# Sliding-window attention and a four-expert mixture: twenty units of the first layer, in place of nine, computed with tokens on partitions

## The chip, the cores and the metric

The kernel runs on one core of a Trainium2 chip. The metric is the device time of one execution in microseconds (us). Three executions of the kernel before took 355.09, 355.31 and 355.94 us; their median is 355.31 us.

## The reference, cut to what matters

```python
B, H, S, D = 4, 8, 768, 64                        # batches, heads, tokens, head width
scores = q @ k.transpose(0, 1, 3, 2) / sqrt(D)
keep   = (pos_k < 4) | ((pos_q - pos_k >= 0) & (pos_q - pos_k < 128))   # 4 sinks, a window of 128
a      = softmax(where(keep, scores, -1e9))
x      = (a @ v).transpose(0, 2, 1, 3).reshape(3072, 512)
p      = domain_probs / (domain_probs.sum(-1) + 1e-9)                   # 3072 x 4
for e in range(4):                                # every token goes through every expert
    out += p[:, e] * (relu(x @ w1[e]) @ w2[e])    # w1: 512 x 1024, w2: 1024 x 512
```

Everything arrives in fp32; the kernel computes its products in bf16 and adds them up in fp32.

## The kernel before, in words

The 3072 tokens are cut into twelve pairs (b, g): batch b (0 to 3), and g (0 to 2) for 256 tokens of it. For each pair there is attention for four pairs of heads, and then the mixture for four experts. A pair and one expert make a unit (b, g, e), 48 of them.

**The first layer.** x @ w1 of a unit is 512 inputs, 1024 outputs and 256 tokens. Most units ("fast" ones, from a start per expert in `START`, all of batches 1 to 3) do it with seven block products in place of eight (a Strassen-Winograd scheme): the operands are cut in halves both ways, and P1, P5, P6, P2, P7, P3 and P4 (the order in which they are issued, `UNITS`) are products of 256 inputs, 512 outputs and 128 tokens. The sums of weight blocks stand in `vf` (`weight_form1`), those of token blocks in `T` (`tokens`); partial sums go through three PSUM banks X, Y and V, with copies on ScalarE (ACT: `seed`, `keep`) and additions on VectorE (DVE).

There are two forms of such a product. In `emit_fast` the weight block is stationary and 128 tokens stream: eight matmuls of 128 columns. The result has hidden units on partitions, and the gate (ReLU times the expert's share of each token) is one DVE instruction with a row of gates that was broadcast to all partitions by a DMA (`gates`, 128 KB, `load_gate`). In `emit_turning` the token block is stationary and 512 weight columns stream: two matmuls of 512 columns, with tokens on partitions. The gate is then one number for each partition (`own_gates`), taken by one DVE instruction, or by two on ACT (ReLU, then a scaling). The result has to be turned before the second layer: when both parts of a half are gated, SyncE (SP) issues a DMA transpose of 128 x 1024 bf16 from a resting tile into H; a unit has two halves, so two transposes. In the kernel before, nine units of the last batch take this form: `TURNED_UNITS = (2, 1)` leaves out the first two and the last one of that batch's twelve. Their resting tiles are taken over from buffers of attention once attention is done (`widened`).

**The second layer** (`emit_product`, line 1463) uses a seven-product scheme as well: for each pair, P1, P2, P6, P5, P7, P3 and P4 over the four experts, four matmuls of 256 columns each; two PSUM banks, emptied by ACT and DVE, stored by SP. P1 and P2 read H itself, P6, P5, P7, P3 and P4 partly sums of its quarters, formed on DVE (`chore`). Units ahead of their expert's start compute the first layer by plain products (line 1092), and pairs (0, 0) and (0, 1) the second layer (line 1549).

**The order of the work.** A planner in the kernel writes out one order for every engine while the program is built. It keeps a clock for each engine (`t`), advances it by modelled durations (`pe`, `act`, `dve`, `sp`), and at each step takes, among the steps that are ready, that with the lowest priority number: an attention step, a product of the first layer, one of the second. Constants such as `SHARE_OF`, `LEAD`, `LOW_PRODUCT` and `FORM` weigh them. Each engine runs its instructions strictly in that order and waits for semaphores where data are missing. Attention of batch b+1 runs among the mixture of batch b. POOL issues the loads of q, k, v and the weights, SP the gates, the transposes and the stores.

Other places that the change touches: `load_v` at the start of the program (line 310; four blocks of the values, issued on POOL ahead of w1 of expert 0, which comes in four quarters, line 323); the division of attention's output by its row sums (lines 790 to 802: four ACT instructions of 64 columns for two heads, or one DVE instruction, line 793, for batch 0); `load_gate` (line 468).

Of the kernel before, what the change touches and what calls it, by code (L numbers as in the profile page):

```python
# [9 lines left out]
ALU = mybir.AluOpType  # L10
AX = mybir.AxisListType
FP32 = mybir.dt.float32
BF16 = mybir.dt.bfloat16
# [3 lines left out]
def kernel(  # L17
# [12 lines left out]
    nc = tc.nc  # L30
# [27 lines left out]
    ]  # L58

    NGATE = 4  # L60
    TURN_ABOUT = 0
# [12 lines left out]
    MASK = 5000  # L74
    GATE = 800
    GATE0 = 300
    FORM = 8000
    TOKEN = 3000
    MARGIN = 0
    HOLD = 0  # L80
    FULL = 7
    STEP0 = 0.01
    READY = 40
    REST = 1500
    LANDS = 0
    WIDE = 2
    OPEN = 2.5
    SOON = 28000
    NEARLY = 2
    ROWED = 24000  # L90
    GATED = 38000
# [306 lines left out]
    def form1_due(e):  # L398
        n = formed1.get(e, 0)
        if e == E - 2 and not (loaded and out_sb):  # L400
            return False
        return landed.get(("w1", e), 1e12) + 3000 < t["pe"] and (n < 3 or n == 3 and not left1[e])

    def form_due(e):
        n = formed.get(e, 0)
        if e == E - 1 and spared_at.get("w2", 1e12) > t["pe"]:
            return False
        return landed.get(("w2", e), 1e12) + 14000 < t["pe"] and (n < 3 or n == 3 and e in used)

    forming = []  # L410

# [38 lines left out]
        dve(2800, 0.0)  # L450

    gate_sb = {}

    def load_gates():

# [284 lines left out]
    def values(b, hp, g):  # L740
# [47 lines left out]
        def run(engine):  # L788
            R = sb.tile([P, 2, 2, 1], FP32, name="R", tag="R", bufs=6)
            nc.vector.reciprocal(out=R, in_=od[:, :, :, D:DX])  # L790
            at = dve(4, fixed=171)
            if b < ONACT:
                nc.vector.tensor_mul(  # L793
                    o[:, :, hp].rearrange("p q (h d) -> p q h d", h=2), od[:, :, :, 0:D], R.to_broadcast([P, 2, 2, D]),
                )
                scaled(dve(2 * P))
                return

            def multiply(engine):
                for qi in range(2):  # L800
                    for ph in range(2):
                        nc.scalar.mul(o[:, qi, hp, ph * D:(ph + 1) * D], od[:, qi, ph, 0:D], R[:, qi, ph])  # L802
# [140 lines left out]
    class Mixture:  # L943


        def __init__(self):
# [34 lines left out]
        def room(self):  # L981
            if self.units and self.units[0] in self.turning and self.halves() < 2:
                return False
            return self.spare or self.live < NH

        def halves(self):
            return sum(x[0] <= t["pe"] + REST for x in self.resting)

# [3 lines left out]
        def widened(self):  # L992

            x = sb.tile([P, 2, NHP, S], BF16, name="qkT", tag="qkT", bufs=1)
            x = x.rearrange("p i h n -> p (i h n)")
            n = 2 * QF * 2 * P
            self.spare = [x[:, i * n:(i + 1) * n].rearrange("p (k f t n) -> p k f t n", k=2, f=QF, t=2) for i in range(3)]
            for tag, bufs, n in (("qkn", NQB, 3), ("onat", 2, 2), ("aT", 4, 1)):
                self.resting += [(t["pe"], sb.tile([P, QF, 2, P], BF16, name="rest", tag=tag, bufs=bufs)) for _ in range(n)]

        def opened(self, b, g, e):

# [10 lines left out]
            def complete(at):  # L1013
                self.H_at[b, g, e] = at
                self.finished.add((b, g, e))
                if (b, g) >= PAIRS[0]:
                    self.waiting.append((b, g, e))
                    load_gates()

            self.H_part[b, g, e] = join(4, complete)  # L1020
            return {"unit": (b, g, e), "fast": fast, "left": list(UNITS) if fast else list(range(QF)), "at": {}}
# [237 lines left out]
        def emit_turning(self, u, m, ready):  # L1259
# [45 lines left out]
            c5 = X[1].rearrange("p f t n -> p (f t n)").bitcast(FP32).rearrange("p (f n) -> p f n", f=QF)  # L1305

            def gated(k, s, src, ready, slack, slot=None, then=None):
                gate = own_gates[:, 2 * g + s, e:e + 1]

                def run(engine):  # L1310
                    if engine == "act":
                        nc.scalar.activation(out=src, in_=src, func=AF.Relu)
                        act(n)
                        nc.scalar.mul(X[k][:, :, s], src, gate)
                        at = act(n)
                    else:
                        nc.vector.tensor_scalar(out=X[k][:, :, s], in0=src, scalar1=0.0, scalar2=gate, op0=ALU.max, op1=ALU.mult)
# [259 lines left out]

    own_gates = consts.tile([P, 2 * NG, E], FP32, name="own_gates")  # L1580
    own_sum = consts.tile([P, 2 * NG], FP32, name="own_sum")

    own_steps = []

    def own_load():
        nc.sync.dma_start(out=own_gates, in_=moe_domain_probs[(B - 1) * S:].rearrange("(t p) e -> p t e", p=P))
        sp()

    def own_made():
# [4 lines left out]
            lambda: nc.vector.tensor_mul(own_gates, own_gates, own_sum[:, :, None].to_broadcast([P, 2 * NG, E])),  # L1594
        ]

        def run(engine):
            steps.pop(0)()
            dve(2 * NG * E)
            own_steps.append(1)  # L1600
            if steps:
                later("dve", t["dve"], 5000, run)
# [30 lines left out]
    while mix.more() or att.more():  # L1633
# [31 lines left out]
        if turns and (ahead < 2 or not mix.second) and landed.get(("qk", *turns[0]), 1e12) < now and (turns[0][0] <= ahead or turns[0][0] == ahead + 1 and not att.todo):  # L1665
# [14 lines left out]
            next_form()  # L1680
        if ahead + 1 < B and not att.more() and (ahead == 0 or (ahead + 1, 0) in turned_at) and (ahead == 0 or mix.done >= sum(work[:ahead]) * LEAD[ahead - 1]):
            ahead += 1
            if ahead == B - 2:
                own_load()
            elif ahead == B - 1:
                own_made()
            att = Attention(ahead)
            upto = mix.done
# [78 lines left out]
```

## Time and profile before

| | |
|---|---|
| median of three executions | 355.31 us |
| the profiled execution: its time | 355.08 us |
| the profiled execution: span from first to last instruction | 353.1 us |
| TensorE (PE) busy | 347.8 us, 98% |
| VectorE (DVE) busy | 295.9 us, 84% |
| ScalarE (ACT) busy | 185.9 us, 53% |
| GpSimd (POOL) busy | 73.7 us, 21% |
| granted TensorE clock | 1.00 throughout |

A row of the groups view has the line, the engine, the operation, its tiles and shapes and its count; then the busy time in us and the mean of one in ns; then the time for which the engine stood idle just before, and what ended that. A matmul's duration counts from its start to the end of its result, so that consecutive matmuls overlap; what one costs the stream is read from the chain of work, where a piece has a start, a length and a number of instructions. The windows view has, for each stretch, the busy time of each engine, the granted clock, the mean share of the DMA engines and the GB/s that they moved.

### The profile page before, as it was taken

To read this page: it belongs to the slowest core of one execution; us is meant where nothing else is said; L and a number is where in the kernel's file an instruction comes from. 1 tells how busy PE (TensorE), PEld (TensorE's weight loads), DVE (VectorE), ACT (ScalarE), POOL (GpSimd) and SP (SyncE) were. 2 spreads that over 40 slices of the span, in tenths; PEclk is the share of its full clock that TensorE was granted. 3 is DMA by queue.
4 is the path that set the end of the run, shared out by engine and by line. 5 is a ranking of instruction groups with operands and counts; after the bars stand their busy time and mean duration, and the time that the engine had idled before them with its cause. 6 is when DMAs were issued, how large, how long until landed. Compare 5 with 4: busy or idle time off the path is not lost.

```text
span 353.1 us, 10221 instructions
## 1 busy us (share of the span) xinstructions
PE 347.8 (98%) x4184; PEld 286.2 (81%) x4184; DVE 295.9 (84%) x690; ACT 185.9 (53%) x459; POOL 73.7 (21%) x91
## 2 busy tenths in 40 slices
PE   8999999999999999999999999999999999999996
PEld 3685769756799998998999898998899675677886
DVE  6787999968999999799899899899789788567640
ACT  5773723438784453647453345555445768826111
POOL 8966114330446206000152000000000000000000
PEclk9999999999999999999999999999999999999999
DMA  9999999999999999810999910131210474736211
GB/s 172 174 190 193 221 217 183 174 159 179 155 142 166 117 197 107 110 63 8 121 158 172 130 53 11 51 88 32 51 59 23 52 121 106 164 89 107 45 62 59
DMA packets 138619, 41.32 MB, mean 117 GB/s; under 512 B 120916, under 2 KB 134580, under 8 KB 138572
## 3 DMA queue, kind: packets, MB, share of 16 engines
q0 software_dynamic: 79104, 17.31, 56.5%
q1 hardware_dynamic: 58412, 22.84, 35.6%
q8 instruction: 32, 0.52, 0.6%
q10 hardware_dynamic: 1056, 0.52, 0.6%
q14 instruction: 15, 0.12, 0.1%
HBM read 39.82 MB, written 6.34 MB: 131 GB/s over the span
## 4 chain that ended last, share of the span: by engine, by line
PE 94%; DVE 2%; DMA 2%; ACT 1%; issue 0%; ACTq 0%; DVEq 0%
PE acc L1463 35%; PE cps L1182 28%; PE acc L1549 8%; PE cps L1294 8%; PE hps L1092 7%; PE sps L697 3%; PE od L763 3%; DMA kraw<-in_k_dram 2%; PE od L756 1%; DVE aT L731 1%; DVE onat L793 1%; PE tx L821 1%; PE tr L594 0%; DVE T L1148 0%; PE sinks L658 0%; ACT aT L722 0%
## 5 line engine op out<-in xcount | busy, mean ns | idle before, releaser
L1463 PEld LDWEIGHTS <-H 128*128 128x128 bf16 x708 | 65.4, 98 | 9.2 <-issue 1.6
L1182 PEld LDWEIGHTS <-w 128*128 128x128 bf16 x992 | 61.5, 98 | 2.3
L722 ACT ACTIVATE aT<-sps 128x512 bf16<-128x512 f32 (+1 forms) x96 | 47.0, 574 | 22.6 <-PE sps L697 22.4
L1463 PE MATMUL acc<-w,H 128*128 128x256 bf16 x420 | 54.9, 273 | 0.0
L1215 DVE SCALAR_TENSOR_TENSOR H<-cps,gates 128x512 bf16<-128x512 f32 x81 | 54.3, 679 | 0.2
L1182 PEld LDWEIGHTS <-vf 128*128 128x128 bf16 x744 | 45.4, 98 | 1.9 <-issue 0.8
L802 ACT ACTIVATE onat<-od,R 128x64 bf16<-128x64 f32 x144 | 33.4, 325 | 17.9 <-DVE R L790 17.6
L1182 PE MATMUL cps<-T,w 128*128 128x128 bf16 x496 | 37.6, 219 | 0.0
L1182 PE MATMUL cps<-xT,w 128*128 128x128 bf16 x496 | 37.3, 219 | 0.0
L1182 PE MATMUL cps<-T,vf 128*128 128x128 bf16 x496 | 36.2, 219 | 0.0
L1463 PEld LDWEIGHTS <-S 128*128 128x128 bf16 x320 | 30.4, 98 | 4.7 <-issue 0.3
L1092 PE MATMUL hps<-xT,w 128*128 128x256 bf16 x256 | 31.8, 273 | 0.1
L1524 ACT COPY osb<-acc 128x256 f32<-128x256 f32 x35 | 13.1, 376 | 35.3 <-PE acc L1463 35.2
L310 POOL DMA_DIRECT2D vx<-in_v_dram x24 | 21.4, 897 | 45.2 <-PE od L763 34.4
L1549 PE MATMUL acc<-w,H 128*128 128x512 bf16 x128 | 29.9, 379 | 0.0
L1228 ACT COPY cps<-cps 128x512 f32<-128x512 f32 x31 | 18.3, 589 | 21.8 <-PE cps L1182 8.4
L1463 PE MATMUL acc<-wf,H 128*128 128x256 bf16 (+1 forms) x216 | 29.0, 271 | 0.0
L1092 PEld LDWEIGHTS <-w 128*128 128x128 bf16 x256 | 24.1, 98 | 4.6 <-issue 0.9
L1235 DVE TENSOR_TENSOR cps<-H,cps 128x512 f32<-128x512 f32 x29 | 20.0, 688 | 7.6 <-PE cps L1182 7.5
L245 POOL DMA_DIRECT2D qkn<-in_q_dram x22 | 19.6, 892 | 22.0 <-DMA qkT<-qkn 13.8
L716 DVE TENSOR_TENSOR aT<-aT,mask 128x1024 bf16<-128x1024 bf16 (+1 forms) x36 | 22.7, 636 | 1.4 <-ACT aT L722 1.3
L1549 PEld LDWEIGHTS <-H 128*128 128x128 bf16 x128 | 12.3, 98 | 12.2 <-issue 0.2
(143 smaller groups left out, 607.1 us busy)
## 6 DMA issues: line engine op xcount, KB each, us to landing
w<-in_moe_w_dram POOLq DMA_DIRECT2D x6, 1024.0 KB, 18.5
out_dram<-osb SPq DMA_DIRECT2D x17, 256.0 KB
gates<-gate_rows SPq DMA_DIRECT2D x31, 128.0 KB
vx<-in_v_dram POOLq DMA_DIRECT2D x24, 128.0 KB, 7.1
qkn<-in_q_dram POOLq DMA_DIRECT2D x22, 128.0 KB, 7.7
qkn<-in_k_dram POOLq DMA_DIRECT2D x22, 128.0 KB, 8.1
w<-in_moe_w_dram POOLq DMA_DIRECT2D x4, 256.0 KB, 7.6
w<-in_moe_w_dram POOLq DMA_DIRECT2D x2, 512.0 KB, 10.9
```

The lines of the kernel that those rows point to most:

```text
L245: nc.gpsimd.dma_start(out=both[:, i], in_=src[b, :, tb * P:(tb + 1) * P, :].rearrange("h p d -> p h d"),)
L310: nc.gpsimd.dma_start(out=vx[tb][:, :, 0:D], in_=v[b, :, tb * P:(tb + 1) * P, :].rearrange("h p d -> p h d"),)
L716: nc.vector.tensor_mul(a, a, m[:, None, :].to_broadcast([P, 2, w]))
L722: nc.scalar.activation(out=a[:, ph], in_=sps[ph][:, 0:w], func=AF.Exp, scale=scale)
L802: nc.scalar.mul(o[:, qi, hp, ph * D:(ph + 1) * D], od[:, qi, ph, 0:D], R[:, qi, ph])
L1092: nc.tensor.matmul(h[:, i].rearrange("p (q n) -> p q n", q=2), lhsT=w1_sb[e][:, db, fb * P:(fb + 1) * P], rhs=xT[b, g][:, :, db], start=(i ...
L1182: nc.tensor.matmul(y[:, f], lhsT=A[:, d, f * P:(f + 1) * P], rhs=T[:, d], start=(m in ("P1", "P5") and f == 0 and d == 0), stop=(d == 1), ...
L1215: nc.vector.scalar_tensor_tensor(out=dst, in0=src, scalar=0.0, in1=gate, op0=ALU.max, op1=ALU.mult)
L1235: nc.vector.tensor_add(tiles["V"], c5, tiles["X"])
L1294: nc.tensor.matmul(y.rearrange("p f n -> p (f n)"), lhsT=T[:, d], rhs=A[:, d], start=(m in ("P1", "P5") and d == 0), stop=(d == 1), skip_g ...
L1463: nc.tensor.matmul(y, lhsT=self.operand(b, g, e, m)[:, f], rhs=forms[e][m][:, f, cs], start=(k == 0 and f == 0 and m in (("P1", "P5", "P2" ...
L1549: nc.tensor.matmul(op, lhsT=H[:, fb // QF, fb % QF, s], rhs=w2_sb[e][:, fb, :], start=(fb == 0), stop=(fb == NFB - 1),)
```

## The change

Twenty units take the tokens-on-partitions form instead of nine: of the 24 units of batches 2 and 3 all but the first four, that is, all of pairs (2, 1) to (3, 2). `own_gates` covers two batches. The gate tiles become two fixed tiles, which serve as resting tiles after the last unit that needs broadcast gates, (2, 0, 3); three more resting tiles come from the q and k buffers as soon as the last batch's q and k are transposed, which is now before attention is over. On ACT the ReLU and the scaling of a gate become two entries of the planner. The division in attention may go to DVE for batches 2 and 3. At the start, the first quarter of w1 is issued between the third and the fourth block of the values. The order of experts changes for five pairs, and some twenty of the planner's constants get other values.

```diff
-    TURNED_UNITS = (2, 1)
-    EXPERTS = {(2, 2): (2, 0, 3, 1)}
+    TURN_ABOUT = 1
+    OWN = 2
+    TURNED_UNITS = (4, 0)
+    EXPERTS = {(1, 0): (0, 2, 1, 3), (1, 1): (3, 2, 1, 0), (1, 2): (3, 2, 1, 0), (2, 2): (2, 0, 3, 1), (3, 1): (3, 2, 1, 0)}
...
-    SHARE_OF = (0.96, 0.92, 0.94)
-    LEAD = (1.01, 1.0)
+    SHARE_OF = (1.01, 0.92, 0.96)
+    LEAD = (1.01, 0.99)
...
-    LOW_PRODUCT = 2.7
+    LOW_PRODUCT = 2.9
...
-    FORM = 8000
+    FORM = 6000
...
-    REST = 1500
+    REST = 3000
...
-    ALONE = 1.3
+    ALONE = 2.0
-    CHORES = 4
+    CHORES = 3
...
+    gate_tiles = [consts.tile([P, 2, 2, P], FP32, name=f"gates{i}") for i in range(NGATE // 2)]
...
-        x = mo.tile([P, 2, P], FP32, name="gates", tag="gates", bufs=NGATE)
+        i = len(gate_sb) % NGATE
+        x = gate_tiles[i // 2][:, i % 2]
...
-    load_v(0, (2, 3))
+    load_v(0, (2,))
     load_w1(0, 4, [0])
+    load_v(0, (3,))
     load_w1(0, 4, [1])
...
             def multiply(engine):
+                if engine == "dve":
+                    nc.vector.tensor_mul(
+                        o[:, :, hp].rearrange("p q (h d) -> p q h d", h=2), od[:, :, :, 0:D], R.to_broadcast([P, 2, 2, D]),
+                    )
+                    scaled(dve(2 * P))
+                    return
...
-            later("act", at, 600, multiply)
+            later("any" if b >= SHARED else "act", at, 600, multiply)
...
-            mine = [u for u in self.order if u[0] == B - 1]
+            mine = [u for u in self.order if u[0] >= OWN]
             self.turning = set(mine[TURNED_UNITS[0]:len(mine) - TURNED_UNITS[1]])
...
+        def rest_gates(self):
+            for x in gate_tiles:
+                self.resting.append((t["pe"], x.rearrange("p i t n -> p (i t n)").bitcast(BF16).rearrange("p (f t n) -> p f t n", f=QF, t=2)))
...
                     if engine == "act":
                         nc.scalar.activation(out=src, in_=src, func=AF.Relu)
-                        act(n)
-                        nc.scalar.mul(X[k][:, :, s], src, gate)
-                        at = act(n)
-                    else:
-                        nc.vector.tensor_scalar(out=X[k][:, :, s], in0=src, scalar1=0.0, scalar2=gate, op0=ALU.max, op1=ALU.mult)
-                        at = dve(n, fixed=152)
+
+                        def scaled(engine):
+                            nc.scalar.mul(X[k][:, :, s], src, gate)
+                            done(act(n))
+                        later("act", act(n), SCALED, scaled)
+                        return
+                    nc.vector.tensor_scalar(out=X[k][:, :, s], in0=src, scalar1=0.0, scalar2=gate, op0=ALU.max, op1=ALU.mult)
+                    done(dve(n, fixed=OWNED_READ))
...
-        nc.sync.dma_start(out=own_gates, in_=moe_domain_probs[(B - 1) * S:].rearrange("(t p) e -> p t e", p=P))
+        nc.sync.dma_start(out=own_gates, in_=moe_domain_probs[OWN * S:].rearrange("(t p) e -> p t e", p=P))
...
+            if b == B - 1 and x[1] == NQB - 1:
+                mix.rest("qkn", NQB, 3, turned_at[x])
```

More of the change, by code (lines that the diff above doesn't have):

```diff
@@ L76 @@
     GATE0 = 300
-    FORM = 8000
+    FORM = 6000
     TOKEN = 3000
-    MARGIN = 0
+    MARGIN = 500
     HOLD = 0
     FULL = 7
-    STEP0 = 0.01
+    STEP0 = 0.03
     READY = 40
-    REST = 1500
+    REST = 3000
     LANDS = 0
+    SCALED = 300
+    SHARED = 2
+    MARGIN1, MARGIN2 = 4000, 14000
+    OWNED_READ = 215
     WIDE = 2
     OPEN = 2.5
-    SOON = 28000
+    SOON = 24000
     NEARLY = 2
@@ L401, in form1_due @@
             return False
-        return landed.get(("w1", e), 1e12) + 3000 < t["pe"] and (n < 3 or n == 3 and not left1[e])
+        return landed.get(("w1", e), 1e12) + MARGIN1 < t["pe"] and (n < 3 or n == 3 and not left1[e])
     def form_due(e):
@@ L407, in form_due @@
             return False
-        return landed.get(("w2", e), 1e12) + 14000 < t["pe"] and (n < 3 or n == 3 and e in used)
+        return landed.get(("w2", e), 1e12) + MARGIN2 < t["pe"] and (n < 3 or n == 3 and e in used)
     forming = []
@@ L984, in room, with rest @@
             return self.spare or self.live < NH
+        def rest(self, tag, bufs, n, at):
+            self.resting += [(at, sb.tile([P, QF, 2, P], BF16, name="rest", tag=tag, bufs=bufs)) for _ in range(n)]
+        def rest_gates(self):
+            for x in gate_tiles:
+                self.resting.append((t["pe"], x.rearrange("p i t n -> p (i t n)").bitcast(BF16).rearrange("p (f t n) -> p f t n", f=QF, t=2)))
         def halves(self):
@@ L997, in widened @@
             self.spare = [x[:, i * n:(i + 1) * n].rearrange("p (k f t n) -> p k f t n", k=2, f=QF, t=2) for i in range(3)]
-            for tag, bufs, n in (("qkn", NQB, 3), ("onat", 2, 2), ("aT", 4, 1)):
-                self.resting += [(t["pe"], sb.tile([P, QF, 2, P], BF16, name="rest", tag=tag, bufs=bufs)) for _ in range(n)]
+            self.rest("onat", 2, 2, t["pe"])
+            self.rest("aT", 4, 1, t["pe"])
         def opened(self, b, g, e):
@@ L1018, in complete @@
                     load_gates()
+                    if not TURNED_UNITS[1] and self.gated[-1] == (b, g, e):
+                        self.rest_gates()
             self.H_part[b, g, e] = join(4, complete)
@@ L1307, in gated @@
             def gated(k, s, src, ready, slack, slot=None, then=None):
-                gate = own_gates[:, 2 * g + s, e:e + 1]
+                gate = own_gates[:, 2 * ((b - OWN) * NG + g) + s, e:e + 1]
                 def run(engine):
@@ L1576, in emit_second @@
                     used.add(e)
-    own_gates = consts.tile([P, 2 * NG, E], FP32, name="own_gates")
-    own_sum = consts.tile([P, 2 * NG], FP32, name="own_sum")
+    OWNED = 2 * NG * (B - OWN)
+    own_gates = consts.tile([P, OWNED, E], FP32, name="own_gates")
+    own_sum = consts.tile([P, OWNED], FP32, name="own_sum")
     own_steps = []
     def own_load():
-        nc.sync.dma_start(out=own_gates, in_=moe_domain_probs[(B - 1) * S:].rearrange("(t p) e -> p t e", p=P))
+        nc.sync.dma_start(out=own_gates, in_=moe_domain_probs[OWN * S:].rearrange("(t p) e -> p t e", p=P))
         sp()
@@ L1682 @@
             ahead += 1
-            if ahead == B - 2:
+            if ahead == 1:
                 own_load()
-            elif ahead == B - 1:
+            elif ahead == 2:
                 own_made()
```

6 lines of the change are left out of this document (3 added, 3 removed).

## The prediction

> **What bounds the kernel now.** I read the page first (busy times, slices, the chain that ended last), then the groups of PE alone, then the chain between two times, then the windows.
>
> ```profile
> span 353.1 us, 10221 instructions
> PE 347.8 (98%) x4184; PEld 286.2 (81%) x4184; DVE 295.9 (84%) x690; ACT 185.9 (53%) x459; POOL 73.7 (21%) x91
> PE   8999999999999999999999999999999999999996
> ...
> PE 94%; DVE 2%; DMA 2%; ACT 1%; issue 0%; ACTq 0%; DVEq 0%
> ...
> L1463 PE MATMUL acc<-w,H 128*128 128x256 bf16 x420 | 54.9, 273 | 0.0
> L1182 PE MATMUL cps<-T,w 128*128 128x128 bf16 x496 | 37.6, 219 | 0.0
> ```
>
> The matmul stream is the kernel: 94% of the chain is PE, and the last number of the group rows, idle time ahead of them, is 0.0. The windows show where PE is not full.
>
> ```profile
> core 0: us, PE busy (x) PEld busy (x) DVE busy (x) ACT busy (x) POOL busy (x), PEclk, DMA share, GB/s
> 0.00:23.00 23.00, 20.58 (x225) 13.30 (x226) 16.89 (x69) 15.84 (x35) 20.74 (x29) 1.00 1.59 180
> 93.00:165.00 72.00, 72.00 (x1031) 65.70 (x1030) 68.51 (x163) 41.01 (x116) 22.48 (x27) 1.00 1.22 121
> 203.00:235.00 32.00, 32.00 (x472) 29.43 (x470) 29.47 (x65) 16.85 (x45) 0.00 (x0) 1.00 0.15 44
> 235.00:264.00 29.00, 29.00 (x426) 26.68 (x424) 25.50 (x56) 15.31 (x42) 0.00 (x0) 1.00 0.20 56
> 264.00:290.00 26.00, 26.00 (x274) 20.25 (x272) 23.17 (x55) 16.49 (x38) 0.00 (x0) 1.00 0.43 63
> 290.00:327.00 37.00, 37.00 (x282) 25.17 (x280) 26.45 (x55) 23.90 (x45) 0.00 (x0) 1.00 0.57 116
> 327.00:353.10 26.10, 23.26 (x232) 20.84 (x229) 10.53 (x28) 3.69 (x11) 0.00 (x0) 1.00 0.18 54
> ```
>
> From 93 to 327 us PE is busy in every microsecond of the quoted stretches, at clock 1.00. Idle time is left only in the first 23 us (2.4 us) and behind the last matmul (2.8 us). So a time can get shorter only by fewer or cheaper matmuls, or at the start; and a wait that the change adds to PE lengthens it, because none is there to be replaced.
>
> **The change, part by part.**
>
> *The eleven further turned units.* The two forms of a product, from the chain (start, length, instructions):
>
> ```profile
> 55.42 8.04 PE cps L1182 x144
> ...
> 279.95 3.88 PE cps L1294 x18
> ...
> 286.00 4.37 PE acc L1463 x40
> ...
> 292.10 3.90 PE cps L1294 x18
> ```
>
> Line 1182 makes 18 products of eight matmuls in 8.04 us, 0.447 each. Line 1294 makes nine products of two matmuls in 3.88 to 3.90 us, 0.431 to 0.433 each. The difference is 0.014 to 0.016 us. Eleven units of seven products are 77 products: 616 matmuls go and 154 come, a saving of 1.05 to 1.2 us; I take 1.15. All of it lies on the path. It is small because the columns streamed are the same, 1024 for a product; only the small cost of a matmul is paid two times instead of eight. (A second-layer product is 4.37 / 10 = 0.437 us, used below.)
>
> The Trainium skill, TensorE: Matmul & The Clock Gate, section Back-to-back issue gap, gives as sustained spacing about 81 ns for 128 columns and 131 ns for 512. By that a product would fall from 0.65 to 0.26 us and the change save some 30 us (an estimate from that page). The trace disagrees, with 56 ns (8.04 / 144) and 216 ns (3.88 / 18), which is near the same section's formula for an isolated matmul.
>
> *What the other engines get.* Durations:
>
> ```profile
> L1215 DVE SCALAR_TENSOR_TENSOR H<-cps,gates 128x512 bf16<-128x512 f32 x81 | 54.3, 679 | 0.2
> L1317 DVE TENSOR_SCALAR rest<-cps,own_gates 128x512 bf16<-128x512 f32 x9 | 6.7, 747 | 1.4 <-PE cps L1294 1.1
> L1317 DVE TENSOR_SCALAR rest<-rest,own_gates 128x512 bf16<-128x512 f32 x9 | 4.3, 480 | 0.1
> L1312 ACT ACTIVATE cps<-cps 128x512 f32<-128x512 f32 x18 | 10.5, 586 | 8.4 <-PE cps L1294 8.2
> L1314 ACT ACTIVATE rest<-cps,own_gates 128x512 bf16<-128x512 f32 x18 | 12.4, 687 | 0.6
> L802 ACT ACTIVATE onat<-od,R 128x64 bf16<-128x64 f32 x144 | 33.4, 325 | 17.9 <-DVE R L790 17.6
> L793 DVE TENSOR_TENSOR onat<-od,R 128x256 bf16<-128x256 f32 x12 | 5.1, 424 | 0.4
> ```
>
> Counted in the built order of the changed kernel: 44 broadcast gates go from DVE (44 x 0.68 = 29.9 us), 5 gates from PSUM (3.7) and 11 from SBUF (5.3) come, and 9 divisions (3.8): 17 us less. ACT gets 28 ReLUs (16.4) and 28 scalings (19.2) and loses 36 divisions (11.7): 24 us more. The new units lie between about 203 and 327 us, where the windows sum to 72.6 us of ACT and 104.6 of DVE in 124. With all the shifts put there, ACT reaches about 97 (78%) and DVE 88 (71%). Neither becomes the bound, and PE gains nothing from a freer DVE, because it does not wait for it now. Priced at nothing; if ACT's queue backs up for a while, the wait comes out in the transposes below.
>
> *Transposes.* 22 more on SP (18 become 40), 11 gate loads fewer. A transpose waits on SP for its gates; behind it in the queue stand stores, which PE does not wait for, and the next transposes, which it does: a weight load of H waits for its half, and all of PE behind it. What a turned unit's way takes, from the last one of before:
>
> ```profile
> 321.90 0.59 PE L1294 MATMUL cps<-vf,xT 128*128 128x512 bf16 x2
> ...
> 323.22 0.59 PE L1294 MATMUL cps<-w,T 128*128 128x512 bf16 x2
> ...
> 323.86 3.37 SPq L1275 DMA_TRANSPOSE qkT<-rest  x2
> ...
> 327.50:328.00 0.50, 0.50 (x6) 0.44 (x5) 0.45 (x1) 0.00 (x0) 0.00 (x0) 1.00 1.10 209
> 328.00:328.50 0.50, 0.50 (x7) 0.45 (x5) 0.45 (x1) 0.00 (x0) 0.00 (x0) 1.00 1.08 198
> 328.50:329.00 0.50, 0.50 (x7) 0.44 (x6) 0.50 (x3) 0.00 (x0) 0.00 (x0) 1.00 0.07 12
> ```
>
> P3 starts at 321.90 and P4 at 323.22, so they have been streamed by 322.33 and 323.65; the second transpose has been issued by 327.23, and the DMA share falls to 0.07 at 328.5. So the later half is there about 4.9 us behind the end of P4 (to 5.4 with the window's width); the earlier half, 1.3 us of issue ahead, about 3.6 behind P4 or 4.9 behind P3.
>
> How long may it take? In the changed PE order I counted the matmuls between a unit's P4 and its first use in the second layer, and weighed them with the lengths above. For the last unit of each pair from (2, 1) to (3, 2), P1 comes 7.1, 8.2, 10.4, 10.4 and 3.9 us behind P4; before, the turned unit with the least distance, (3, 2, 2), had 14.9. P1 needs the earlier half, P2, 1.75 us later, the other. So for (3, 2, 3), 3.9 against 3.6 and 5.7 against 4.9: just enough, with 0.3 to 0.8 us to spare; the others have more. I price it at 0; the ends are 0 and 2.5 us (below).
>
> *The start.* Rows around the first read of w1:
>
> ```profile
> 7.42 1.76 POOL L310 DMA_DIRECT2D vx<-in_v_dram  x2
> 9.16 3.16 POOL L323 DMA_DIRECT2D w<-in_moe_w_dram  x4
> ...
> DMA to landing us min/median/max: 6.6/6.6/6.6
> ...
> 15.79 0.68 PE L697 MATMUL sps<-qkT 64*128 64x128 bf16 x6
> 16.40 0.39 PE L573 MATMUL acc<-lent 128*128 128x256 bf16 x2
> 16.63 1.04 PE L1092 MATMUL hps<-xT,w 128*128 128x256 bf16 x8
> ...
> 17.93 0.23 PE L756 MATMUL od<-vsd,sinkA 128*128 128x130 bf16 x1
> ...
> 17.60 2.15 ACT L722 ACTIVATE aT<-sps 128x512 bf16<-128x512 f32 x4
> ```
>
> The first quarter (issued at 9.16, landed 6.6 later, 15.8) moves ahead of one block of values, 1.76 / 2 = 0.88 us earlier: 14.9. The fourth block is issued one quarter's 0.79 us later and lands near 15.7; its first reader is behind 17.93, so that costs nothing. The changed order puts the first group of line 1092 straight behind the sinks, drops the two idle products of 16.40 (0.23 us) and joins two single score steps into a pair. But the value products wait for ACT's exponentials, which end at 19.75 either way. So the gain lies between 0 and about 0.5 us (the idle products and one more switch); I take 0.2. A quarter that lands later than 14.9, with PE now waiting for it at 15.8 and no idle product in between, could cost 0.3.
>
> *At nothing:* the planner's constants and the experts' order. The matmul counts of attention and of the second layer are unchanged, and so is the number of blocks of score matmuls (30). PE's full stretch hides changes of place; without that cover each late operand would be paid in full. Sooner resting tiles and the two fixed gate tiles wait for regions, not for a whole tile; their first uses wait for loads as before.
>
> *The sum.* Against the profiled execution (355.08, its span 353.1 and 1.98 around it): 355.08 - 1.15 - 0.2 = 353.73. The median of the runs lies 0.23 above it: 353.96, so 354.0.
>
> **The rivals.**
>
> *Slower: the turned halves come late.* Place: the weight loads of P1 and P2 of the last unit of a pair, (3, 2, 3) above all. For it speaks that both of its last gates are on ACT (1.27 us a gate in place of 0.75 on DVE), that SP is strictly in order, and that it has waited long ahead of a transpose:
>
> ```profile
> L1275 SPq EVENT_SEMAPHORE x18: 17/17/4142, 273.4 to 325.9; - x18
> ```
>
> Were 4.1 us put into the way of (3, 2, 3), 4.9 + 4.1 stands against 5.7, 3.3 us late; with 0.4 at (2, 1), where 9.0 meets 8.9, the time is 354.0 + 3.7 = 357.7, and with half of it 355.8. It decides from 2.4 us late (355.31 + 1.07 - 354.0), that is, a way of 8.1 us. Against it: no store stands between those two transposes and the unit's P4 in SP's order. Chance 0.17.
>
> The Trainium skill, Advanced Engine Details and Errata, section X-Bar Transpose (TRN2), expects 350 to 400 GB/s, by which one transpose of 256 KB moves in about 0.7 us (an estimate). The trace has 198 to 209 GB/s, so the way is not that short here.
>
> *No difference.* The start gives nothing, since ACT ends it, and small waits of 0.1 to 0.3 us at a few of the new first reads eat half of the 1.15: 355.31 - 0.6 = 354.7, with 354.3 to 355.3 around it. For it speaks how little there is to gain; against it, that PE now waits at none of the first reads of nine units, though these have 14.9 us and more. Chance 0.25.
>
> *Far faster.* What a product costs is set by its number of matmuls, each with a weight load, and not by its columns: at line 1182's 0.056 us, 462 fewer are worth 25.8 us, and the time is 329.5. The nine turned units of before speak against it: they are in the new form already, and take 0.216 us a matmul. Chance 0.01. The rule cited above from the Trainium skill's page on TensorE is of this kind and would end near 325 us.
>
> **How the numbers follow.** The forecast (353.4 to 354.2) has 0.57, and the rest is above. A change of 0.3%, 1.07 us, is about what can be told from none; the forecast, 1.3 us, is only just beyond it. Faster 0.57 + 0.01 = 0.58, same 0.25, slower 0.17. The range goes from 353.1 (both gains at their upper ends, 1.2 and 0.5, and 0.5 for smaller waits at switches) to 356.6, where the lateness is some 2.6 us; outside lie the worse half of the slow case and little below.
>
> **What would show it.** Lines move: 1182, 1294, 1463 and 1092 become 1205, 1317, 1490 and 1115. Right: 280 matmuls in line 1317, two in 0.432 us, and 1120 in line 1205; PE full in all windows up to its last products; line 1115 first near 15.8. Wrong: idle time ahead of line 1490's weight loads, released by a DMA into H or qkT, most of all near the end; or ACT above 90% of the windows from 203 on, with gates late there.

## The result, and the profile after

| | before | changed |
|---|---|---|
| median of twelve executions each, side by side | 355.14 us | 354.32 us (354.01 to 354.58) |
| the profiled execution: its time | 355.08 us | 354.29 us |
| its span | 353.1 us | 352.6 us |
| its last matmul starts at | 350.04 us | 349.18 us |

The ratio is 0.9973 with a 95% interval of 0.9964 to 0.9981: 0.82 us less, where the forecast was 354.0 and 1.3 us less. The gain is clear of the noise, but it stays just inside the 0.3% that the prediction called no change. The last matmul starts 0.86 us earlier, yet the span is only 0.5 us shorter: from that start to the last instruction it takes 3.4 us in place of 3.1, and why was not looked into. All ratios compare fast executions alone; only e5_w2at4 and e6_t2w4, below, had slow ones, two of six each, which their medians include.

From the page of the changed kernel: the span, the busy times, the shares of the chain that ended last, and three groups.

```profile
span 352.6 us, 9354 instructions
...
PE 346.6 (98%) x3720; PEld 266.8 (76%) x3720; DVE 283.0 (80%) x671; ACT 209.6 (59%) x479; POOL 74.4 (21%) x91
...
PE 75%; DMA 20%; POOL 4%; issue 0%; ACT 0%; DVE 0%; POOLq 0%; SPq 0%
...
L816 ACT ACTIVATE onat<-od,R 128x64 bf16<-128x64 f32 x108 | 24.9, 325 | 11.4 <-DVE R L798 11.1
...
L1338 ACT ACTIVATE rest<-cps,own_gates 128x512 bf16<-128x512 f32 x36 | 24.8, 692 | 0.7
...
L1317 PE MATMUL cps<-w,T 128*128 128x512 bf16 x80 | 23.8, 379 | 0.0
```

Each form sits in the program as forecast: 80 matmuls in this group of line 1317 (280 in the line), none waiting, and 36 divisions fewer on ACT. DVE lost 13 us (forecast 17) and ACT gained 24 (forecast 24). New is the chain that ended last: 20% of it is DMA, where before it was 2%. One wait of 0.25 us at 86.7 us, shown below, is enough to lead it back into the loads. The windows, with the columns of the prediction's:

```profile
93.00:165.00 72.00, 72.00 (x1026) 65.39 (x1025) 69.21 (x167) 41.06 (x116) 23.32 (x26) 1.00 1.23 118
...
203.00:235.00 32.00, 32.00 (x317) 23.27 (x315) 25.50 (x58) 20.85 (x48) 0.00 (x0) 1.00 0.32 67
235.00:264.00 29.00, 29.00 (x246) 19.26 (x244) 23.22 (x54) 21.50 (x42) 0.00 (x0) 1.00 0.52 105
264.00:290.00 26.00, 26.00 (x198) 17.41 (x197) 19.64 (x52) 21.02 (x41) 0.00 (x0) 1.00 0.76 134
290.00:327.00 37.00, 37.00 (x257) 24.89 (x255) 23.30 (x50) 27.26 (x50) 0.00 (x0) 1.00 0.55 111
```

PE is full in these windows from 93 to 327 us, as before, and ACT is at 81% in its fullest one (21.02 of 26). The only wait of PE that the waits view names between 23 us and the end is this (engine, tile and line, releaser; us in total, times, longest); the timeline shows its place:

```profile
PE sinks L666 <- DMA qkT<-qkn: 0.2, 1, 0.2
```

```profile
86.71 0.29 PE L666 MATMUL sinks<-qkT,ksd 128*32 128x256 bf16 x4 [0.25 <-DMA qkT<-qkn]
```

Three places of the kernel before:

```profile
86.66 0.29 PE L658 MATMUL sinks<-qkT,ksd 128*32 128x256 bf16 x4
...
160.91 0.62 PE L697 MATMUL sps<-qkT 64*128 64x128 bf16 x12
...
349.87 0.39 PE L1463 MATMUL rest<-qkn,qkT 128*128 128x128 bf16 x4
```

and two of the changed kernel:

```profile
161.19 0.62 PE L705 MATMUL sps<-qkT 64*128 64x128 bf16 x12
...
349.01 0.39 PE L1490 MATMUL rest<-qkn,H 128*128 128x128 bf16 x4
```

Before, the sinks of batch 1 started at 86.66, with no wait. So these two executions are level there, although that of the changed kernel had run 0.67 us ahead at its first sinks (14.76 against 15.43; over all profiles these start at 14.7 to 14.8 or at 15.2 to 15.5 us, in programs that are the same up to there, too). The score steps of the two kernels follow one another in the same order up to 161 us. Between 86.7 and 161.2 us the changed kernel falls another 0.23 us behind: the block of scores at 160.91 before stands at 161.19. From there to the last matmul it gains 1.14 us and ends 0.86 ahead.

### The profile page after: what moved, and what is told of

Same layout as the page of the kernel before. It is cut to its first block, busy times and chain, and to the rows that moved or that the text cites. A ratio compares the mean times of both kernels' runs of the same rounds, so it can differ in the third digit from the quotient of the medians.

```text
span 352.6 us, 9354 instructions
## 1 busy us (share of the span) xinstructions
PE 346.6 (98%) x3720; PEld 266.8 (76%) x3720; DVE 283.0 (80%) x671; ACT 209.6 (59%) x479; POOL 74.4 (21%) x91
## 4 chain that ended last, share of the span: by engine, by line
PE 75%; DMA 20%; POOL 4%; issue 0%; ACT 0%; DVE 0%; POOLq 0%; SPq 0%
PE acc L1490 35%; PE cps L1317 17%; PE cps L1205 15%; DMA w<-in_moe_w_dram 8%; DMA qkn<-in_q_dram 5%; DMA qkn<-in_k_dram 4%; DMA qkT<-qkn 3%; PE sps L705 3%; PE od L771 2%; POOL qkn L250 2%; PE hps L1115 1%; PE od L764 1%; POOL vx L315 1%; POOL w L338 0%; PE acc L1576 0%
## 5 line engine op out<-in xcount | busy, mean ns | idle before, releaser
L1490 PEld LDWEIGHTS <-H 128*128 128x128 bf16 x708 | 66.6, 98 | 17.9 <-issue 1.3
L1205 PEld LDWEIGHTS <-w 128*128 128x128 bf16 x640 | 39.2, 98 | 1.2 <-issue 0.5
L1238 DVE SCALAR_TENSOR_TENSOR H<-cps,gates 128x512 bf16<-128x512 f32 x54 | 36.4, 680 | 0.0
L1335 ACT ACTIVATE cps<-cps 128x512 f32<-128x512 f32 x46 | 26.6, 585 | 16.2 <-PE cps L1317 15.6
L1205 PEld LDWEIGHTS <-vf 128*128 128x128 bf16 x480 | 29.3, 98 | 1.0 <-issue 0.5
L1115 PEld LDWEIGHTS <-w 128*128 128x128 bf16 x256 | 24.0, 98 | 5.2 <-issue 1.5
L1338 ACT ACTIVATE rest<-cps,own_gates 128x512 bf16<-128x512 f32 x36 | 24.8, 692 | 0.7
L1205 PE MATMUL cps<-T,w 128*128 128x128 bf16 x320 | 24.3, 219 | 0.0
L1205 PE MATMUL cps<-xT,w 128*128 128x128 bf16 x320 | 24.1, 219 | 0.0
L1317 PE MATMUL cps<-w,T 128*128 128x512 bf16 x80 | 23.8, 379 | 0.0
L1317 PE MATMUL cps<-vf,T 128*128 128x512 bf16 x80 | 23.6, 379 | 0.0
```

The costliest lines, as they stand in the source:

```text
L1115: nc.tensor.matmul(h[:, i].rearrange("p (q n) -> p q n", q=2), lhsT=w1_sb[e][:, db, fb * P:(fb + 1) * P], rhs=xT[b, g][:, :, db], start=(i ...
L1205: nc.tensor.matmul(y[:, f], lhsT=A[:, d, f * P:(f + 1) * P], rhs=T[:, d], start=(m in ("P1", "P5") and f == 0 and d == 0), stop=(d == 1), ...
L1238: nc.vector.scalar_tensor_tensor(out=dst, in0=src, scalar=0.0, in1=gate, op0=ALU.max, op1=ALU.mult)
L1317: nc.tensor.matmul(y.rearrange("p f n -> p (f n)"), lhsT=T[:, d], rhs=A[:, d], start=(m in ("P1", "P5") and d == 0), stop=(d == 1), skip_g ...
L1490: nc.tensor.matmul(y, lhsT=self.operand(b, g, e, m)[:, f], rhs=forms[e][m][:, f, cs], start=(k == 0 and f == 0 and m in (("P1", "P5", "P2" ...
```

## The experiments

Each run stands against the kernel before beside it on the same chip:

| run | what is done | median, us | before, us | ratio (95%) |
|---|---|---|---|---|
| e1_old_start | changed, old start | 354.07 | 355.25 | 0.9968 (0.9957 to 0.9980) |
| e2_before_new_start | before, new start alone | 355.16 | 355.25 | 0.9995 (0.9986 to 1.0004) |
| e3_split8 | turned products in eight matmuls | 356.65 | 355.25 | 1.0042 (1.0029 to 1.0055) |
| e4_nine | changed, nine units turned | 355.89 | 355.25 | 1.0014 (1.0005 to 1.0022) |
| e10_old_const | changed, old constants | 354.96 | 355.12 | 0.9998 (0.9989 to 1.0007) |
| e11_nine_old_const | nine units, old constants | 355.36 | 355.12 | 1.0005 (0.9996 to 1.0014) |
| e7_act_div | all divisions on ACT | 355.50 | 355.12 | 1.0011 (1.0003 to 1.0020) |
| e9_last | last unit's transposes twice | 359.26 | 355.12 | 1.0130 (1.0109 to 1.0152) |
| e8_double | all transposes of H twice | 441.64 | 355.15 | 1.2429 (1.2406 to 1.2452) |
| e5_w2at4 | w2 of expert 3 issued later | 364.88 | 355.15 | 1.0233 (1.0192 to 1.0275) |
| e6_t2 | 22 units turned | 356.04 | 355.15 | 1.0017 (1.0007 to 1.0028) |
| e6_t2w4 | the last two together | 365.63 | 355.15 | 1.0247 (1.0203 to 1.0292) |

Below, a difference from the changed kernel is that of the two differences from before: for e3_split8 +1.40 against -0.82, so 2.2 us.

### What the form of a product saves

```diff
             for d in range(2):
-                nc.tensor.matmul(y.rearrange("p f n -> p (f n)"), lhsT=T[:, d], rhs=A[:, d], ...)
+                for f in range(QF):
+                    nc.tensor.matmul(y[:, f], lhsT=T[:, d], rhs=A[:, d, f * P:(f + 1) * P], ...)
```

> The changed kernel, each product of the tokens-on-partitions form issued as eight matmuls of 128 columns in place of two of 512; gates, transposes and the order stay. If the small cost of a matmul is what the form saves: 140 products x 0.0154 us = 2.2 us more, 356.5 us. If the form's worth comes from elsewhere (VectorE relieved, other places of the waits): no change, 354.3 us.

Measured: 2.2 us more than the changed kernel, for 140 products with six matmuls more each: 0.016 us a product. The same seven products stand in the chain of both, first of the changed kernel, then of this one (start, length, instructions):

```profile
229.04 3.03 PE cps L1317 x14
```

```profile
229.60 3.13 PE cps L1318 x56
```

3.03 / 7 is 0.433 us, 3.13 / 7 is 0.447. The columns set most of the price; four times the matmuls, each with its weight load, cost 3% more. This is what the turned form saves: 140 products at the longer price cost more than the changed kernel's whole gain. Whether it is the matmul or its weight load that costs, no run separates.

### The start

```diff
 e1_old_start, in the changed kernel:
-    load_v(0, (2,))
-    load_w1(0, 4, [0])
-    load_v(0, (3,))
+    load_v(0, (2, 3))
+    load_w1(0, 4, [0])
 e2_before_new_start: the reverse, in the kernel before
```

> The changed kernel with the old start: both blocks of values ahead of the first quarter of w1. Theory A (the loads of the first 86 us set the pace up to the first sinks of batch 1, which wait for a transpose of batch 1's q and k, so that a gain at the start is lost there): 354.3 us, as the changed kernel, and that sinks group stands near 86.7 us again. Theory B (the new start carries its 0.2 to 0.3 us to the end): 354.5 to 354.6 us, with the later groups of matmuls shifted by as much.

> The kernel before with the new start alone. Theory A: 355.1 us, no change, the first sinks of batch 1 near 86.7 us. Theory B: 354.8 to 354.9 us.

Measured: the old start is no worse in the changed kernel (0.9968 against 0.9973, the intervals overlap), and the new start alone does nothing that can be told to the kernel before. Theory A has the nearer time in both. The timeline of PE in e2_before_new_start shows where it goes:

```profile
15.43 0.43 PE L659 MATMUL sinks<-qkT,ksd 128*32 128x256 bf16 x4
15.79 1.05 PE L1093 MATMUL hps<-xT,w 128*128 128x256 bf16 x8
...
17.57 0.38 PE L698 MATMUL sps<-qkT 64*128 64x128 bf16 x5 [0.28 <-ACT aT L723]
17.88 0.23 PE L757 MATMUL od<-vsd,sinkA 128*128 128x130 bf16 x1
```

The edit does what it says: the first group of w1 runs at 15.79 instead of 16.63, and the idle products are gone. But PE then waits 0.28 us for ACT's exponentials to free a place for scores, and the first value product starts at 17.88, where it started at 17.93. Later, at 86.7 us, PE meets the transposed q and k of batch 1. The chain of the changed kernel runs through the loads up to there (start, length):

```profile
29.01 28.43 DMA w<-in_moe_w_dram
...
60.59 14.97 DMA qkn<-in_k_dram
...
75.61 10.97 DMA qkT<-qkn
```

It ends in the sinks of 86.71, shown above. Leaving out the runs that load w2 later, the profiles reach this place between 86.45 and 87.00 us. Four of them were some 0.7 us ahead of the kernel before at the first sinks. The changed kernel, e4_nine and e10_old_const then wait here 0.17 to 0.25 us for the transposes; e8_double does not. All four are left with 0.2 us of that lead or with none. The others, at 86.64 to 87.00, do not wait. So PE and the loads arrive within a few tenths of a microsecond of one another, and of a start that is 0.7 us faster at most 0.2 us is seen behind this place.

### The planner's constants

```diff
 e4_nine:
-    TURNED_UNITS = (4, 0)
+    TURNED_UNITS = (14, 1)
 e10_old_const (e11_nine_old_const: both):
-    SHARE_OF = (1.01, 0.92, 0.96)
+    SHARE_OF = (0.96, 0.92, 0.94)
 ... LEAD, LOW_PRODUCT, FORM, MARGIN, STEP0, REST, SOON, ALONE, CHORES and EXPERTS as in the kernel before
```

> The changed kernel with nine turned units of the last batch as before, and all else of the change kept (planner's constants, start, fixed gate tiles, division on either engine). If the turned units carry the gain: 77 products x 0.0154 us = 1.2 us more than the changed kernel, 355.3 to 355.6 us, so nothing is left of the gain. If the constants or the start carry a part: 354.5 to 354.9 us.

> The changed kernel (twenty turned units, gates on ACT in two entries, shared divisions, new start) with the old values of the planner's constants and the old order of experts. Theory A (the constants only move small waits about, as the prediction priced them): 353.8 to 354.7 us, the same number of matmuls. Theory B (the constants are what lets the turned units keep their saving; without them halves or gates are late): 355.2 us or more, with waits of PE of 1 us and more in sum between 203 and 345 us.

> The nine units of before in the changed program, as in the run with nine units, and the old values of the constants and order of experts on top. That run was 0.64 us above the kernel before. Theory A (the new constants, fitted to twenty units, cost nine units those 0.64 us): 354.9 to 355.4 us, level with before. Theory B (the new parts of the program cost them: the ACT gate in two entries, divisions on DVE, resting tiles): 355.6 to 356.1 us as with the new constants.

Measured: e4_nine is 0.64 us above before, above both of its expectations. With the old constants as well (e11, in theory A's range), 0.24 of it is left, with an interval that takes in none. Twenty units with the old constants (e10) come to 0.16 under before, which can't be told from nothing: the constants are worth 0.66 us of the changed kernel's 0.82. By the intervals of the ratios, each such difference of two runs is uncertain by some 0.4 us. Neither theory of e10 names its time: it lies between both. Its chain shows two short waits where the changed kernel has none:

```profile
268.59 0.59 ACT cps L1357
...
307.31 0.70 DVE cps L1364
```

A copy of a PSUM bank on ACT and an addition on DVE end late by 0.39 and 0.27 us (the gaps between the starts of PE's matmuls less their usual distance). e4_nine has three, of 0.27, 0.31 and 0.23 us, behind two such additions and behind a scaling of a gate on ACT (line 1338); e11 has one of 0.45, behind an addition of line 1364. The rows of e4_nine's chain:

```profile
280.31 0.70 DVE cps L1364
...
295.80 0.70 ACT rest L1338
...
332.57 0.70 DVE cps L1258
```

So by the medians the new constants suit twenty units (0.66 us better) and cost nine units 0.40, which is no more than the uncertainty. In e10, e4_nine and e11 one to three short waits of 0.4 to 0.8 us in sum appear. They need not come from the constants: e11 has the old count and the old constants together, and its wait must come from the other parts of the change. (Ten constants and the order of experts differ, not some twenty constants.) The turned units by themselves are worth 1.46 us with the new constants (e4_nine to the changed kernel) and 0.40 with the old (e11 to e10), where the matmul count says 1.19.

### ACT against DVE

```diff
-    SHARED = 2
+    SHARED = 4
```

> The changed kernel with all divisions of attention on ACT, as before (no sharing with DVE): ACT gets some 8 us more in the last two batches' stretch, where it has 20.9 to 27.3 us of work in windows of 26 to 37 us. Theory A (ACT's load is no bound, as the prediction has it): 354.0 to 354.7 us. Theory B (ACT's queue backs up and gates come late at the turned units): 355.0 us or more, with waits of PE released by ACT or by DMA H<-rest.

Measured: 1.2 us more than the changed kernel, as much as the turned form saves. The time is theory B's; the waits are not where theory B had them, since none is released by ACT or by DMA H<-rest. Which groups move, from 203 to 352 us, first in the changed kernel, then here:

```profile
L1335 ACT ACTIVATE cps<-cps 128x512 f32<-128x512 f32 x46 | 26.6, 585 | 16.2 <-PE cps L1317 15.6
...
L1342 DVE TENSOR_SCALAR rest<-cps,own_gates 128x512 bf16<-128x512 f32 x7 | 5.2, 749 | 2.0 <-PE cps L1317 2.0
...
L816 ACT ACTIVATE onat<-od,R 128x64 bf16<-128x64 f32 x12 | 2.8, 324 | 0.0
```

```profile
L1335 ACT ACTIVATE cps<-cps 128x512 f32<-128x512 f32 x40 | 23.5, 591 | 17.4 <-PE cps L1317 17.0
L816 ACT ACTIVATE onat<-od,R 128x64 bf16<-128x64 f32 x48 | 11.1, 332 | 0.4 <-DVE R L798 0.3
L1342 DVE TENSOR_SCALAR rest<-cps,own_gates 128x512 bf16<-128x512 f32 x10 | 7.5, 749 | 2.2 <-PE cps L1317 2.1
```

Divisions on ACT (48 for 12) drive six gates from ACT to DVE (three more in the row of line 1342, three more in its sister row that writes into `gates`). ACT's idle time does not shrink, and neither engine is near full: between 203 and 327 us ACT has 90.2 us of work and DVE 90.6, of 124. Still PE waits, by 0.19, 0.29, 0.26 and 0.27 us at 215, 244, 271 and 333 us, 1.0 us together. These are the distances between the starts of its matmuls less the usual ones (0.44 less 0.15 at 244, behind a score step); a row shows less, since the ends of matmuls overlap what follows. The profile names a releaser for one alone, that at 244:

```profile
244.13 0.59 PE L1317 MATMUL cps<-w,T 128*128 128x512 bf16 x2 [0.23 <-DVE cps L1364]
```

DVE's addition of line 1364 started at 243.39, behind a gate on DVE (line 1342) that had started at 242.72. What ends 0.3 us late at one place costs that, whatever the averages are. What was late at the other three is not shown.

### The transposes

```diff
 e8_double; e9_last only for (b, g, e) == (3, 2, 3):
-    nc.sync.dma_start(out=H[:, k]..., in_=X[k]..., transpose=True)
+    for _ in range(2):
+        nc.sync.dma_start(out=H[:, k]..., in_=X[k]..., transpose=True)
```

> The changed kernel with every transpose of a turned half issued twice (80 in place of 40; the second writes the same data again, and readers wait for it). The matmul order is the same. If only the way to the last unit is near its limit: the later half of (3, 2, 3), issued from 335.9 and landed by 339.1 in the changed kernel, has two more issues of 1.26 us ahead of its last one and lands near 340.5 to 341.2, against a read at 340.0; so a wait of 0.4 to 1.2 us there, none in the other pairs, 354.7 to 355.5 us. If SP and the transfers of the transposes are already a load that PE feels in all pairs: waits at several first reads, 356.5 us or more.

> The changed kernel with both transposes of its last unit, (3, 2, 3), issued twice to the same place; the other 38 once. The second of a half waits on SP for the landing of the first. In the changed kernel the halves were moved at 335.3 to 336.7 and 337.0 to 338.6 us, and were first read at 338.28 (P1) and 340.03 (P2). Theory A (the place that the prediction named for the slower rival has almost no cover, and a late half is paid in full): with a second landing some 2.5 us later for the first half and twice that for the second half, P1 starts at about 339.8 and P2 some 3.5 to 4 us later than before: 357.0 to 358.6 us, with one or two waits of PE on DMA H<-rest as the only new ones. Theory B (PE has other products to run there, or the landing that PE waits for is that of the first transpose): under 355 us.

e8_double is some 80 us beyond anything that was expected; the "356.5 us or more" takes it in by its words alone. The second transpose writes where the first does, and it waits on SP, by a semaphore, until the first has landed. SP's timeline (start, length) of one unit, in the changed kernel and here:

```profile
334.14 2.97 SPq L1298 DMA_TRANSPOSE H<-rest  x2
```

```profile
216.13 8.87 SPq L1299 DMA_TRANSPOSE H<-rest  x4
```

Forty halves at 8.87 / 2 = 4.4 us are 177 us of SP, more than the 124 us from 203 to 327. PE then waits for DVE, which in its turn waits for the halves that it has to sum (waits view, PE's two longest and DVE's longest):

```profile
PE acc L1491 <- DVE osb L1541: 29.7, 4, 11.5
PE cps L1318 <- DVE cps L1365: 25.6, 9, 7.4
DVE S L1432 <- DMA H<-rest: 48.7, 10, 8.7
```

It says what becomes of a full SP, not what one late half costs. e9_last does. In the changed kernel the way of that unit was (PE's timeline, then DVE's):

```profile
333.92 0.59 PE L1317 MATMUL cps<-w,T 128*128 128x512 bf16 x2
...
338.28 1.04 PE L1490 MATMUL acc<-w,H 128*128 128x256 bf16 x8
...
340.03 0.60 PE L1490 MATMUL acc<-w,H 128*128 128x256 bf16 x4
```

```profile
339.12 0.43 DVE L1431 TENSOR_TENSOR S<-H 128x512 bf16<-128x512 bf16 x1 [3.27 <-DMA H<-rest]
```

P4 is followed by the first reads of P1 (338.28) and P2 (340.03), and DVE, which waited for the later half, gets it at 339.1. In e9_last:

```profile
340.68 1.47 PE L1491 MATMUL acc<-w,H 128*128 128x256 bf16 x8 [2.05 <-DMA H<-rest]
341.94 1.91 PE L1491 MATMUL acc<-w,qkT 128*128 128x256 bf16 x8
345.05 0.61 PE L1491 MATMUL acc<-w,H 128*128 128x256 bf16 x4 [1.20 <-DMA H<-rest]
```

In the chain of e9_last three landings of 3.05 to 3.21 us and one issue of 1.24 follow one another, from 334.32 to 345.00. P2 starts 5.02 us later than in the changed kernel, and the last matmul 5.03 later (354.21): theory A, at 359.26 us even above its 357.0 to 358.6, because a second landing had been put at 2.5 us and takes some 3. With its second transpose the later half is there at 345.00 in place of 339.1, 5.9 us later; P2 pays for all of it but the 0.9 us that it had to spare.

### Further versions

```diff
 e5_w2at4 (e6_t2w4: both):         e6_t2:
-    W2AT = 2                      -    TURNED_UNITS = (4, 0)
+    W2AT = 4                      +    TURNED_UNITS = (2, 0)
```

> The changed kernel with the load of the last expert's w2 (1 MB) issued behind four blocks of batch 1's q and k in place of two. If the loads set the pace up to the first sinks of batch 1 (near 86.7 us): the wait there for a transpose goes, that stretch of PE gets 0.25 to 0.4 us shorter, 353.9 to 354.1 us. If it was not the loads: the wait stays or another operand is as late, 354.3 us.

> The changed kernel with 22 turned units in place of 20. By matmul counts 14 products x 0.0154 us = 0.2 us less, 354.1 us. The plan has one extra matmul of 512 columns (0.22 us) and more units turned while attention of the last batch still runs: if new waits come with that, 354.3 us or more.

> Both of the two edits before it: 22 turned units and the later load of the last w2. If they add: 353.7 to 353.9 us.

None was faster. e5_w2at4 and e6_t2w4 are far above their expectations, and of e6_t2 the second branch holds, with new waits. Issuing w2 of expert 3 later, to let batch 1's q and k land sooner, removes the wait at the sinks but makes w2 itself late. The waits of e5_w2at4 and of e6_t2:

```profile
PE acc L1576 <- DMA w<-in_moe_w_dram: 3.0, 1, 3.0
PE od L771 <- DVE aT L724: 2.3, 1, 2.3
```

```profile
PE cps L1324 <- ACT onat L816: 0.7, 1, 0.7
PE sps L705 <- ACT rest L1338: 0.4, 1, 0.4
```

In this one trial the order of the loads had no slack to give; others were not tried. Two stretches at half the clock, shown at the end, add to e5's time. Two units more save 0.2 us of matmuls, which the extra matmul takes back, and put 1.1 us of waits behind ACT's divisions and gates, while attention still runs; e6_t2 is 1.7 us above the changed kernel, so some 0.6 us are not named. No version was shown to beat the changed kernel; e1_old_start is level with it.

## Why the prediction was right, and where it was not

**What bounds the kernel: right.** PE stayed full at clock 1.00 and its matmuls set the end. The waits that experiments added to it came out in the time: 1.0 us of them in e7_act_div for 1.2 us, 5.0 us in e9_last for 5.0.

**The turned units, 1.15 us: right.** The mean distance of undisturbed matmuls is 55.9 ns in line 1205 and 215.9 in line 1317, so 77 products save 77 x (8 x 0.0559 - 2 x 0.2159) = 1.19 us; by e3_split8, 77 x 0.016 = 1.2. Behind 161 us, where all of the new turned units lie, the changed kernel gains 1.14. The rival that counts matmuls alone (329.5 us) is refuted by the same run. The rule of the Trainium skill, TensorE: Matmul & The Clock Gate, section Back-to-back issue gap (some 81 ns for 128 columns, 131 for 512), is not borne out by this trace, with 56 and 216.

**The start, 0.2 us: wrong, it is 0.** The step that failed is "the idle products and one more switch": they lay beside the wait for ACT's exponentials, as the rival of no difference had it, and e2 shows them turned into a wait of 0.28 us: the first value product starts 0.05 us earlier, not 0.2.

**"At nothing: the planner's constants and the experts' order": wrong in size.** The constants are a term of their own: without them 0.66 us are gone (e10), as much as its two waits of 0.39 and 0.27. "PE's full stretch hides changes of place" was no ground: PE was full in these runs, and each late operand lengthened it.

**A term that the prediction does not have: 0.33 us.** In the changed kernel small delays (0.1 us each among the value products at 103 us and the scores at 141) make 0.05 + 0.23 = 0.28 us by 161 us, and 1.19 - 1.14 = 0.05 go behind it: -1.19 + 0.33 = -0.86, which is the shift of the last matmul. These 0.33 and the missing 0.2 are what the forecast has too much. The new constants carry little of it. From the sinks of batch 1 to the score block at 161 us it is 74.25 us before (86.66 to 160.91) and 74.48 in the changed kernel (86.71 to 161.19), but 74.41 already in both runs with the old constants (e10, 86.47 to 160.88; e11, 86.64 to 161.05). So 0.16 of the 0.23 comes with the rest of the change, and which part of that, stays open.

**"Neither becomes the bound", ACT and DVE at nothing: right in the outcome, weak in the reason.** ACT reached 90.6 us and DVE 91.7 between 203 and 327 us, near the 97 and 88 foretold. But e7_act_div has nearly the same sums and is 1.2 us slower. The shares could not tell; with the divisions on DVE, priced in the prediction only as a part of a sum, PE had no wait above 0.15 us from 203 us on, and with them on ACT it had four of 0.19 to 0.29.

**The transposes: right, and the 4.9 us partly by luck.** The later half of (3, 2, 3) was foretold 4.9 us behind the end of P4. P4 had been streamed by 333.92 + 0.43 = 334.35, and the half was there at 339.1: 4.8. But the prediction ended the way where the transfer ends. Here that is at 338.3 (193 to 216 GB/s until then, 387 behind it, where a store runs), only 3.9 behind P4, and DVE was released 0.8 later. So the way was about 1 us shorter than that of the unit it was read from, and the time from the transfer's end to the release, which the prediction left out, makes up for it. P2 read the half 5.7 us behind P4, as counted. Nothing waited, with 0.9 us to spare; e9_last shows that the slower rival had its place right, and that beyond those 0.9 us all is paid for. It did not happen: SP had nothing ahead of these transposes. (In that rival's sum, 9.0 against 8.9 is 0.1 us late and not 0.4, so its time would be 357.4; nothing hangs on it.) The transfer, at 199 to 216 GB/s in half-microsecond windows while it ran alone, is again below the 350 to 400 GB/s of the Trainium skill, Advanced Engine Details and Errata, section X-Bar Transpose (TRN2).

What stays open: which of the constants carries the 0.66 us, which part of the change delays the stretch up to 161 us by 0.16, and why the gain of eleven units is 1.46 us with one set of constants and 0.40 with the other, beyond the short waits named and the uncertainty of 0.4.

## What to carry to other kernels

When one engine is full from end to end, price every moved step by the time its result has to spare, place by place; the busy shares of the other engines (73% here) do not tell whether a 0.3 us wait appears. Fewer, longer matmuls over the same columns saved only their small fixed part, here 3% of a product. So the rest of the schedule had to be fitted to the change: with the old constants nothing of it could be told from none. A gain ahead of a point that waits for loads can be lost there: of 0.7 us at most 0.2 was kept.

## What the runs showed of the hardware

Two things were not expected. A DMA transpose that overwrites the target of one just issued waited on its queue for that one's landing: in e9_last a landing came 3.05 to 3.21 us after the start of an issue that takes 1.23 us itself, and nothing behind it on SP started meanwhile. And the granted clock fell after PE had stood still, not while it did. In e9_last's windows (the clock stands behind the five busy times) it is 1.00 through the wait of 2.05 us and for the first half microsecond of matmuls, then 0.50 for 3.4 us, then 1.00 again, also behind the next wait, of 1.20 us. The eight matmuls of line 1491 at 341.94 took 1.91 us, where they took 1.04 in the changed kernel. The last row is from e5_w2at4, where PE had waited 3.03 us until 83.25; the other such stretch there is from 121.66 to 125.08.

```profile
338.00:340.60 2.60, 0.63 (x6) 0.31 (x4) 0.00 (x0) 0.00 (x0) 0.00 (x0) 1.00 0.78 150
340.60:341.14 0.54, 0.47 (x5) 0.42 (x6) 0.00 (x0) 0.00 (x0) 0.00 (x0) 1.00 1.13 208
341.15:344.56 3.41, 2.70 (x14) 1.56 (x11) 0.00 (x0) 0.37 (x1) 0.00 (x0) 0.50 0.48 103
345.00:346.00 1.00, 0.95 (x9) 0.87 (x10) 0.87 (x3) 0.00 (x0) 0.00 (x0) 1.00 0.73 277
...
84.12:87.53 3.41, 3.41 (x16) 1.76 (x15) 0.75 (x1) 0.57 (x1) 0.00 (x0) 0.50 2.80 142
```

Not every such wait is followed by a fall: in e6_t2w4 one of 2.24 us until 83.14 was not (clock 1.00 from 80 to 92 us), and one of 2.34 us until 118.96 was (0.50 from 119.93 to 123.33).
